# Pooled attention with a token-mixing layer on one core: PSUM banks chosen by expected release, wider sums of exponentials, two key buffers

## The chip, the cores and the metric

One core of a Trainium2 chip runs the whole program. Its engines work side by side and wait for each other by semaphores: TensorE (PE, with its weight loads listed as PEld), VectorE (DVE), ScalarE (ACT), GpSimd (POOL), and SyncE (SP), which here only starts transfers. The metric is the device time of one execution in microseconds; less is better.

## The reference

```python
q_pool = q.reshape(B, H, S // 2, 2, D).mean(axis=3)          # B, H = 8, 8; S = 1152; D = 64
scores = q_pool @ k^T / sqrt(D)                              # per head 576 x 1152
scores = scores - max(scores, axis=-1)
attn = exp(scores);  attn = attn / (sum(attn, -1) + 1e-9)
x = attn @ v, heads side by side                             # (8, 576, 512)
theta = x @ w_theta
y = w_tok_r @ (x * cos(theta)) + w_tok_i @ (x * sin(theta))  # over the 576 tokens
u = x + y
out = u + relu(u @ w_ch)
```

## The kernel before

The first stage is the attention. It goes over 32 pairs of heads (`NPAIR`), two heads side by side in the 128 partitions. A pair has two halves of the pooled queries (u = 0, 1; 288 columns each) and nine key tiles (kt = 0 to 8). What is done for a pair i:

- `load_q`, `load_k`, `load_v` start the transfers of queries, keys and values; `pool_q` (GpSimd) adds neighbouring queries.
- `prep_t` turns keys and pooled queries on TensorE (tiles `pt`, twice a pair, g = 0 and 1); `prep_hi` (ScalarE) and `prep_lo` (VectorE) split the result in two parts `hi` and `lo`.
- `maxpass` computes rough scores on TensorE (`pm`, twelve tiles a pair) and VectorE reduces each to maxima (L312). `max_tail` does the rest (`px`), `max_nm` and `max_row` (`pmt`, `mT`) turn the maxima, and `load_max` writes them as a row (`nmr`) by four small transfers.
- `escore` computes the exact scores for one u and kt in eight matmuls (`pe`, with the maximum subtracted in the fourth term), and ScalarE takes the exponential into `pc` (L374).
- `ssum` adds exponentials of kt = 0 to 7 on GpSimd (L383, `ss`); that of kt = 8 (`TAIL`) stays apart.
- `av` multiplies the exponentials with the values (`pa`, nine key tiles, two heads). `norm_sum` sums over the keys by matmuls with ones (L408). The `norm_` steps invert the sums by way of DRAM, multiply, and store.

Between these, `weights` fetches the 18 tiles of the later stage's weights step by step: several VectorE operations (L525 to L540), GpSimd (L542, L544, L555), and for token weights a turn on TensorE into `pwt` with splits by ScalarE and VectorE (L161, L164). The second stage (x to out, 8 batches) is left as it is.

The order on every engine is written by hand. Each step has a position in units of one `escore` (18 to a pair), in tables such as `PLAN`, `MAX_AT`, `AV_AT` and `W_AT`; all steps are sorted by it and each engine then takes them in that order. `burst(i, 0)` at position 10.35 holds the second `prep_all` of pair i+2, `max_row` of the next, `av`, and `norm_sum` of the pair before; `burst(i, 1)` at 19.25 holds `tail_prep` and the other `av`.

Results of matmuls go to PSUM, taken in double banks by `bank2`. There are four: two of kind "e" for `pe` and `pa`, two of kind "m" for all else, each kind used in turn. There are 14 buffers for exponentials and one for the keys (`kn`).

Of the kernel before, what the change touches and what calls it, by code (L numbers as in the profile page):

```python
# [9 lines left out]
F32 = mybir.dt.float32  # L10
# [7 lines left out]
EPS = 1e-9  # L18
TAIL = 8
PC_BUFS = 14  # L20
MAX_AT = (-24.9, -23.65, -22.55, -20.85, -19.55, -18.8, -15.55, -14.35, -13.5, -11.6, -10.2, -9.15)
# [10 lines left out]
    "load_q": -44.55,  # L32
    "load_k": -43.2,
    "pool_q": -35.35,
# [12 lines left out]
BANKS = {}  # L47
PAIRS = {"e": 2, "m": 2}
BANKS2 = {"h": 1, "t": 1, "m": 4, "r": 2}
# [42 lines left out]
def pooled_attention_moe_kernel(  # L92
# [51 lines left out]
    def bank(kind, name):  # L144
        pool, bufs = psum["now"]
        return pool.tile([P, 512], F32, tag=kind, name=name, bufs=bufs[kind])

    def bank2(kind, name):
        return psum["now"][0].tile([P, 2, 512], F32, tag=kind, name=name, bufs=PAIRS[kind])

# [37 lines left out]
    with ExitStack() as p1:  # L188
# [3 lines left out]
        )  # L192
        inp = p1.enter_context(tc.tile_pool(name="inp", bufs=1))
        opd = p1.enter_context(tc.tile_pool(name="opd", bufs=3))
# [26 lines left out]
        def load_k(i):  # L221
            b, hp = divmod(i, NP)
            h0 = 2 * hp
            kn = inp.tile([P, KT, 2, D], F32, tag="kn", name=f"kn{i}")
            for h in range(2):
                nc.sync.dma_start(kn[:, :, h, :], k[b, h0 + h].rearrange("(p t) d -> p t d", t=KT))
            state[i]["kn"] = kn
# [8 lines left out]
        def load_v(i):  # L236
            b, hp = divmod(i, NP)
            h0 = 2 * hp
            vn = inp.tile([P, 2, KT, D], F32, tag="vn", name=f"vn{i}", bufs=2)
            nc.sync.dma_start(vn, v[b, h0 : h0 + 2].rearrange("h (p t) d -> p h t d", t=KT))  # L240
            state[i]["vn"] = vn
# [10 lines left out]
        def prep_t(i, g):  # L252
            st = state[i]
            kn = st["kn"]
            pt = st["pt", g] = bank2("m", f"pt{g}_{i}")
            if g == 0:
# [39 lines left out]
        def maxpass(i):  # L296
# [4 lines left out]
            for j in range(4):  # L301
                for g in range(3):
                    pm = bank2("em"[g % 2] if i == 0 else "m", f"pm{i}_{j}{g}")
                    for h, hs in enumerate(HEADS):
                        nc.tensor.matmul(  # L305
                            pm[:, h, 0:W],
                            hi[hs, Q0 + j * P : Q0 + (j + 1) * P],
                            hi[hs, K0[3 * g] : K0[3 * g] + W],
                            start=True,
                            stop=True,  # L310
                        )
                    nc.vector.tensor_reduce(  # L312
                        mx[:, j : j + 5 : 4, g : g + 1], pm[:, :, 0:W], AX.X, ALU.max
                    )
                    yield

        def max_tail(i, pt):
            st = state[i]
            hi, tl, mx = st["hi"], st["tail"], st["mx"]
            pm = bank2("m", f"px{i}")  # L320
            for n, c, k, w in ((0, 0, 0, 4), (1, 0, 4, 2), (1, 2 * P, 6, 2)):
# [4 lines left out]
            if pt is None:  # L326
                pt = bank2("m", f"py{i}")
            nc.tensor.matmul(
# [10 lines left out]
        def max_row(i):  # L339
            st = state[i]  # L340
            px = bank2("m", f"pmt{i}")
            nc.tensor.transpose(out=px[0:KT, 0, 0:P], in_=st["nm"], identity=ident)
            mT = st["mT"] = sml.tile([KT, P], F32R, tag="mT", name=f"mT{i}")
            nc.scalar.copy(mT, px[0:KT, 0, 0:P])
            return px

# [7 lines left out]
        def escore(i, u, kt):  # L354
            st = state[i]
            hi, lo, nmr = st["hi"], st["lo"], st["nmr"]
            pcs = st.setdefault("pc", {})
            pcs[u, kt] = pch.tile([P, 2, HALF], F32, tag="pc", name=f"pc{i}_{u}{kt}")
            pe = bank2("e", f"pe{i}_{u}{kt}")
# [16 lines left out]
        def ssum(i, u, kt):  # L376
            st = state[i]
            if kt == 0 or kt >= TAIL:
                return
            if kt == 1:  # L380
                st["ss", u] = nrm.tile([P, 2, HALF], F32, tag=f"ss{u}", name=f"ss{u}_{i}", bufs=2)
            first = st["pc"][u, 0] if kt == 1 else st["ss", u]
            nc.gpsimd.tensor_tensor(st["ss", u], first, st["pc"][u, kt], ALU.add)  # L383

        def av(i, u):
            st = state[i]
            if u == 0:
                st["xu"] = nrm.tile([P, 2, HALF], F32, tag="xu", name=f"xu{i}", bufs=3)
            pa = bank2("e", f"pa{i}_{u}")
            for kt in range(KT):  # L390
# [10 lines left out]
        def norm_sum(i, px):  # L401
            st = state[i]
            sets = [[st["ss", u]] + [st["pc"][u, kt] for kt in range(TAIL, KT)] for u in range(2)]
            for n in range(len(sets[0])):
# [51 lines left out]
        def burst(i, u):  # L456
            if u == 0:
                if i + 2 < NPAIR:
                    prep_all(i + 2, 1)
                px = max_row(i + 1) if i + 1 < NPAIR else bank2("m", f"pmt{i}")  # L460
                av(i, u)
                if i > 0:
                    norm_sum(i - 1, px)
            else:
# [31 lines left out]
        def weights():  # L496
# [78 lines left out]
            def token(wv, kb, jt):  # L575
# [8 lines left out]
                yield  # L584
                pw2 = bank2("m", "pwt")
                pt = pw2[:, 0]
# [37 lines left out]
        def early():  # L624
            run(wgen)
            pw.close()
            xp0 = ctx.enter_context(tc.tile_pool(name="xp0", bufs=1, side="right"))
            xTs.append(xp0.tile([P, ND, 5 * P], F32, name="xT0"))
# [55 lines left out]
        for i in range(NPAIR):  # L684
            plan(i)
        at(NU * NPAIR + 2, 9, lambda: norm_sum(NPAIR - 1, bank2("m", "pend")))
        pw = ExitStack()
# [303 lines left out]
```

## Time and profile before

| | us |
|---|---|
| median of 3 runs | 1422.26 |
| lowest and highest | 1418.68, 1423.93 |
| span of the profiled execution, first to last instruction | 1414.8 |
| VectorE busy | 862.2 |
| ScalarE busy | 730.6 |
| GpSimd busy | 911.4 |

The time of the profiled execution outside its span is not listed; the median of the runs is 7.5 us more than the span. The attention takes the first 920 us of the span. A matmul row's length is from its start to its modelled end, and rows of neighbours overlap, so the start-to-start distance tells what an instruction costs TensorE.

### The profile page before, as it was taken

To read this page: it belongs to the slowest core of one execution; us is meant where nothing else is said; L and a number is where in the kernel's file an instruction comes from. 1 tells how busy PE (TensorE), PEld (TensorE's weight loads), DVE (VectorE), ACT (ScalarE), POOL (GpSimd) and SP (SyncE) were. 2 spreads that over 40 slices of the span, in tenths; PEclk is the share of its full clock that TensorE was granted. 3 is DMA by queue.
4 is the path that set the end of the run, shared out by engine and by line. 5 is a ranking of instruction groups with operands and counts; after the bars stand their busy time and mean duration, and the time that the engine had idled before them with its cause. 6 is when DMAs were issued, how large, how long until landed. Compare 5 with 4: busy or idle time off the path is not lost.

```text
span 1414.8 us, 29922 instructions
## 1 busy us (share of the span) xinstructions
PE 1352.8 (96%) x12178; PEld 1086.1 (77%) x12178; DVE 862.2 (61%) x1143; ACT 730.6 (52%) x1250; POOL 911.4 (64%) x672
## 2 busy tenths in 40 slices
PE   5999999999999999999999999999999999999998
PEld 4667676766676767767776766688999999999998
DVE  5866676777577767766687666355362553536442
ACT  2556465655555655556565655465444544445431
POOL 2789888978798889889898888834232413232210
PEclk7999999999999999999999999999999999999999
DMA  5224343434342443324343421231111211111111
GB/s 127 74 75 126 85 111 84 119 85 116 86 125 69 108 122 106 94 83 125 84 111 86 119 80 51 79 122 38 35 38 34 60 50 34 38 35 44 28 31 38
DMA packets 130906, 111.66 MB, mean 79 GB/s; under 512 B 95040, under 2 KB 95424, under 8 KB 130768
## 3 DMA queue, kind: packets, MB, share of 16 engines
q1 hardware_dynamic: 130592, 109.28, 28.0%
q8 instruction: 96, 1.57, 0.5%
q0 software_dynamic: 176, 0.46, 0.1%
q14 instruction: 42, 0.34, 0.1%
HBM read 88.29 MB, written 21.27 MB: 77 GB/s over the span
## 4 chain that ended last, share of the span: by engine, by line
PE 67%; DVE 15%; ACT 10%; DMA 3%; issue 3%; POOL 1%; SPq 0%; ACTq 0%; POOLq 0%; DVEq 0%
PE pa L392 16%; PE pe L371 16%; PE py L821 11%; PE pth L743 7%; PE pr L860 5%; DVE mx L312 5%; ACT pc L374 4%; PE pm L305 3%; PE pt L265 3%; PE pmt L408 2%; DMA kn<-in_k_dram 2%; DVE wf L532 1%; PE pxn L731 1%; DVE ws L530 1%; DVE lo L292 1%
## 5 line engine op out<-in xcount | busy, mean ns | idle before, releaser
L383 POOL TENSOR_TENSOR ss<-ss,pc 128x576 f32<-128x576 f32 x384 | 558.1, 1453 | 98.2 <-ACT pc L374 75.9
L312 DVE TENSOR_REDUCE mx<-pm 128x2 f32<-128x768 f32 x384 | 343.9, 950 | 134.8 <-PE pm L305 134.4
L374 ACT ACTIVATE pc<-pe 128x576 f32<-128x576 f32 x576 | 371.2, 652 | 102.2 <-PE pe L371 84.2
L392 PE MATMUL pa<-pc,vn 128*64 128x288 f32 x2304 | 293.5, 409 | 0.3 <-ACT pc L374 0.3
L794 POOL TENSOR_TENSOR Z<-ab,Z 128x512 fp32r<-128x512 f32 x40 | 52.2, 1305 | 306.0 <-ACT Z L790 277.8
L392 PEld LDWEIGHTS pa<-pc,vn 128*64 128x64 f32 x2304 | 159.7, 137 | 110.7 <-ACT pc L374 4.8
L821 PE MATMUL py<-wtk,Z 128*128 128x288 f32 x1728 | 241.7, 297 | 0.0
L821 PEld LDWEIGHTS py<-wtk,Z 128*128 128x128 f32 x1728 | 233.2, 189 | 1.3
L371 PE MATMUL pe<-hi 64*128 64x288 f32 x1152 | 203.1, 349 | 14.9 <-ACT pc L374 6.5
L371 PEld LDWEIGHTS pe<-hi 64*128 64x128 f32 x1152 | 108.3, 184 | 92.9 <-ACT pc L374 57.9
L371 PE MATMUL pe<-hi,lo 64*128 64x288 f32 x1152 | 170.8, 293 | 0.0
L371 PE MATMUL pe<-lo,hi 64*128 64x288 f32 x1152 | 170.8, 293 | 0.0
L371 PE MATMUL pe<-nmr,oner 64*128 64x288 f32 x1152 | 169.5, 290 | 0.0
L305 PE MATMUL pm<-hi 64*128 64x384 f32 x768 | 138.1, 359 | 14.6 <-DVE mx L312 8.6
L371 PEld LDWEIGHTS pe<-lo,hi 64*128 64x128 f32 x1152 | 109.8, 187 | 0.0
L371 PEld LDWEIGHTS pe<-hi,lo 64*128 64x128 f32 x1152 | 109.1, 186 | 0.0
L371 PEld LDWEIGHTS pe<-nmr,oner 64*128 64x128 f32 x1152 | 109.0, 185 | 0.0
L292 DVE TENSOR_TENSOR lo<-pt,hi 128x768 fp32r<-128x768 f32 x64 | 67.6, 1057 | 66.9 <-ACT hi L281 66.9
L860 PEld LDWEIGHTS pr<-us,wch 128*128 128x128 f32 x768 | 104.5, 188 | 2.0
L860 PE MATMUL pr<-us,wch 128*128 128x288 f32 x768 | 105.8, 295 | 0.0
L281 ACT CAST hi<-pt 128x768 fp32r<-128x768 f32 x64 | 56.2, 878 | 91.5 <-DVE mx L332 74.3
L383 POOL TENSOR_TENSOR ss<-pc,pc 128x576 f32<-128x576 f32 x64 | 93.8, 1466 | 3.0 <-ACT pc L374 3.0
(105 smaller groups left out, 1652.7 us busy)
## 6 DMA issues: line engine op xcount, KB each, us to landing
qn<-in_q_dram SPq DMA_DIRECT2D x32, 576.0 KB
kn<-in_k_dram SPq DMA_DIRECT2D x64, 288.0 KB
vn<-in_v_dram SPq DMA_DIRECT2D x32, 576.0 KB
dn<-ro SPq DMA_DIRECT2D x64, 144.0 KB
xd<-xu SPq DMA_DIRECT2D x32, 288.0 KB
xT<-xd SPq DMA_DIRECT2D x8, 1152.0 KB
out_dram<-on SPq DMA_DIRECT2D x23, 192.0 KB
out_dram<-on SPq DMA_DIRECT2D x23, 128.0 KB
```

The costliest lines, as they stand in the source:

```text
L281: nc.scalar.copy(hi, src)
L292: nc.vector.tensor_tensor(lo, src, hi.bitcast(F32), ALU.subtract)
L305: nc.tensor.matmul(pm[:, h, 0:W], hi[hs, Q0 + j * P : Q0 + (j + 1) * P], hi[hs, K0[3 * g] : K0[3 * g] + W], start=True, stop=True,)
L312: nc.vector.tensor_reduce(mx[:, j : j + 5 : 4, g : g + 1], pm[:, :, 0:W], AX.X, ALU.max)
L371: nc.tensor.matmul(pe[:, h, 0:HALF], w[hs], x[hs], start=(n == 0), stop=(n == 3))
L374: nc.scalar.activation(pcs[u, kt], pe[:, :, 0:HALF], AF.Exp, scale=SC)
L383: nc.gpsimd.tensor_tensor(st["ss", u], first, st["pc"][u, kt], ALU.add)
L392: nc.tensor.matmul(pa[hs, 0, 0:HALF], st["vn"][:, h, kt, :], st["pc"][u, kt][:, h, :], start=(kt == 0), stop=(kt == KT - 1),)
L743: nc.tensor.matmul(th, xs[c][:, j * P : (j + 1) * P], ws[:, c], start=(n == 0), stop=(n == 11))
L794: engine("zlo", b).tensor_tensor(Z[1], t, Z[0].bitcast(F32), ALU.subtract)
L821: nc.tensor.matmul(st["py", c, u][:, 0:HALF], Z[zi][:, c * P : (c + 1) * P], wtk[wi][:, kw, u * HALF : (u + 1) * HALF], start=(i == 0 and ...
L860: nc.tensor.matmul(pr[u][:, 0:HALF], wch[wi][:, c, e * P : (e + 1) * P], st["us", ui][:, c, u * HALF : (u + 1) * HALF], start=(n == 0), st ...
```

## The change

Three things change, all in the attention stage.

Banks: the two kinds are given up. A planner in `bank2` keeps a clock for TensorE, ScalarE and VectorE, and for each of four double banks the time at which it expects it free. Each tile takes the bank that comes free first. For each kind of tile `HOLD` has the TensorE work, the engines that read it (a: ScalarE, d: VectorE), and the time from then to its release. The order of work on the engines stays.

Sums: exponentials of an even and the following odd key tile now lie in one buffer (seven such buffers), that of kt = 8 in one of its own (`pl`, three buffers). GpSimd adds whole buffers, so that `ss` holds two sums side by side, and `norm_sum` sums three pieces by the ones matmul instead of two. `norm_sum` takes a bank of its own (`pns`) and doesn't share that of `max_row`.

Keys: there are two `kn` buffers, and `load_k` goes from position -43.2 to -43.62, ahead of `load_max`. The pool of the inputs goes to the other side of SBUF; `vn` changes its pool.

```diff
-TAIL = 8
-PC_BUFS = 14
+PC_BUFS = 7
-    "load_k": -43.2,
+    "load_k": -43.62,
-PAIRS = {"e": 2, "m": 2}
+SLOTS = 4
+HOLD = {
+    "e": (0.54, "a", 0.6),
+    "pm": (0.17, "d", 0.95),
+    "pt": (0.75, "ad", 2.1),
+    "px": (0.6, "d", 1.55),
+    "pa": (4.4, "a", 0.4),
+    "mt": (0.2, "a", 0.3),
+    "ns": (1.5, "a", 0.5),
+    "pw": (0.75, "ad", 1.9),
+}
...
+    clock = {"p": 0.0, "a": 0.0, "d": 0.0}
+    slots = [0.0] * SLOTS
     def bank2(kind, name):
-        return psum["now"][0].tile([P, 2, 512], F32, tag=kind, name=name, bufs=PAIRS[kind])
+        n = min(range(SLOTS), key=lambda k: slots[k])
+        work, engines, after = HOLD[kind]
+        clock["p"] = max(clock["p"], slots[n]) + work
+        end = max([clock["p"] + 0.3] + [clock[e] for e in engines]) + after
+        for e in engines:
+            clock[e] = end
+        slots[n] = end + 0.1
+        return psum["now"][0].tile([P, 2, 512], F32, tag=f"b{n}", name=name, bufs=1)
...
-            kn = inp.tile([P, KT, 2, D], F32, tag="kn", name=f"kn{i}")
+            kn = inp.tile([P, KT, 2, D], F32, tag="kn", name=f"kn{i}", bufs=2)
...
-            pcs[u, kt] = pch.tile([P, 2, HALF], F32, tag="pc", name=f"pc{i}_{u}{kt}")
+            if kt == KT - 1:
+                pcs[u, kt] = pch.tile([P, 2, HALF], F32, tag="pl", name=f"pl{i}_{u}", bufs=3)
+            elif kt % 2 == 0:
+                pw2 = st["pp", u, kt] = pch.tile([P, 2, 2, HALF], F32, tag="pc", name=f"pc{i}_{u}{kt}")
+                pcs[u, kt], pcs[u, kt + 1] = pw2[:, 0], pw2[:, 1]
...
-            if kt == 0 or kt >= TAIL:
+            if kt < 3 or kt % 2 == 0:
                 return
-            if kt == 1:
-                st["ss", u] = nrm.tile([P, 2, HALF], F32, tag=f"ss{u}", name=f"ss{u}_{i}", bufs=2)
-            first = st["pc"][u, 0] if kt == 1 else st["ss", u]
-            nc.gpsimd.tensor_tensor(st["ss", u], first, st["pc"][u, kt], ALU.add)
+            if kt == 3:
+                st["ss", u] = nrm.tile([P, 2, 2, HALF], F32, tag="ss", name=f"ss{u}_{i}", bufs=3)
+            first = st["pp", u, 0] if kt == 3 else st["ss", u]
+            nc.gpsimd.tensor_tensor(st["ss", u], first, st["pp", u, kt - 1], ALU.add)
...
-            sets = [[st["ss", u]] + [st["pc"][u, kt] for kt in range(TAIL, KT)] for u in range(2)]
+            sets = [[st["ss", u][:, n] for n in range(2)] + [st["pc"][u, KT - 1]] for u in range(2)]
```

Each call of `bank2` now names its kind of `HOLD`: "e" in `escore`, "pa" in `av`, "pm" in `maxpass`, and so on.

On SP, around the maxima of one pair (`nmr`), with the store of a finished pair (`xd`) and the loads behind it. Before:

```order
L351 DMA nmr_109<-mT_3580 1x4x128
L352 DMA nmr_109<-mT_3580 1x16x4
L351 DMA nmr_109<-mT_3580 1x4x128
L352 DMA nmr_109<-mT_3580 1x16x4
L491 DMA xd_83<-xu_2801 128x576
L226 DMA kn_3620<-in_k_dram 128x9x64 x2
L240 DMA vn_3634<-in_v_dram 128x2x576
```

and in the changed kernel:

```order
L246 DMA kn_3517<-in_k_dram 128x9x64 x2
L370 DMA nmr_109<-mT_3479 1x4x128
L371 DMA nmr_109<-mT_3479 1x16x4
L370 DMA nmr_109<-mT_3479 1x4x128
L371 DMA nmr_109<-mT_3479 1x16x4
L515 DMA xd_83<-xu_2722 128x576
L260 DMA vn_3537<-in_v_dram 128x2x576
```

The load of keys moved from behind the four transfers of the maxima and the store to ahead of them all.

On GpSimd, the sums of pair 9 with the pooling of queries (`qp`) and a weight step between them. Before:

```order
L383 TENSOR_TENSOR ss_9_3872<-ss_9_3872,pc_07_3890 128x576
L542 TENSOR_TENSOR raw<-raw 128x512
L383 TENSOR_TENSOR ss_9_4077<-pc_10_3922,pc_11_3941 128x576
L383 TENSOR_TENSOR ss_9_4077<-ss_9_4077,pc_12_4012 128x576
L383 TENSOR_TENSOR ss_9_4077<-ss_9_4077,pc_13_4035 128x576
L383 TENSOR_TENSOR ss_9_4077<-ss_9_4077,pc_14_4051 128x576
L544 TENSOR_TENSOR ws<-wf,raw 128x512
L383 TENSOR_TENSOR ss_9_4077<-ss_9_4077,pc_15_4066 128x576
L234 TENSOR_TENSOR qp_4140<-qn_3935 96x6x64 x2
L383 TENSOR_TENSOR ss_9_4077<-ss_9_4077,pc_16_4079 128x576
L555 TENSOR_TENSOR hl<-ws,hl 128x512
L383 TENSOR_TENSOR ss_9_4077<-ss_9_4077,pc_17_4095 128x576
```

and in the changed kernel:

```order
L406 TENSOR_TENSOR ss_9_3790<-ss_9_3790,pc_06_3765 128x1152
L566 TENSOR_TENSOR raw<-raw 128x512
L406 TENSOR_TENSOR ss_9_3996<-pc_10_3811,pc_12_3904 128x1152
L568 TENSOR_TENSOR ws<-wf,raw 128x512
L406 TENSOR_TENSOR ss_9_3996<-ss_9_3996,pc_14_3942 128x1152
L254 TENSOR_TENSOR qp_4026<-qn_3824 96x6x64 x2
L579 TENSOR_TENSOR hl<-ws,hl 128x512
L406 TENSOR_TENSOR ss_9_3996<-ss_9_3996,pc_16_3967 128x1152
```

Seven adds of a half became three of twice the width, and the first of them now needs the exponentials of four key tiles instead of two.

On TensorE, the ones matmul for pair 8 behind `pa` of pair 9, with `pe` of the next key tile behind it. Before:

```order
L408 MATMUL pmt_3966<-ss_8_3485,ones 32x288
L408 MATMUL pmt_3966<-ss_8_3687,ones 32x288
L408 MATMUL pmt_3966<-ss_8_3485,ones 32x288
L408 MATMUL pmt_3966<-ss_8_3687,ones 32x288
L408 MATMUL pmt_3966<-pc_08_3519,ones 32x288
L408 MATMUL pmt_3966<-pc_18_3721,ones 32x288
L408 MATMUL pmt_3966<-pc_08_3519,ones 32x288
L408 MATMUL pmt_3966<-pc_18_3721,ones 32x288
L371 MATMUL pe_12_4013<-hi_2992 128x288 x2
```

and in the changed kernel:

```order
L431 MATMUL pns_3879<-ss_8_3617,ones 32x288
L431 MATMUL pns_3879<-ss_8_3414,ones 32x288
L431 MATMUL pns_3879<-ss_8_3617,ones 32x288
L431 MATMUL pns_3879<-pl_0_3420,ones 32x288
L431 MATMUL pns_3879<-pl_1_3619,ones 32x288
L431 MATMUL pns_3879<-pl_0_3420,ones 32x288
L431 MATMUL pns_3879<-pl_1_3619,ones 32x288
L394 MATMUL pe_12_3905<-hi_2910 128x288 x2
```

Eight matmuls became twelve (the first five of the changed kernel, on `ss` too, are left out above), and their bank is no longer that of `pmt`.

## Rows read from the trace of the kernel before

**Rows 1.** The page: the span, and in the 40 equal slices of the span the busy share of TensorE in tenths.

```profile
span 1414.8 us, 29922 instructions
PE   5999999999999999999999999999999999999998
```

**Rows 2.** The chain of waits through one pair, from 700 to 729 us: start, length, what. `x8` counts matmuls of one `pe`, `x16` eight matmuls with their eight weight loads.

```profile
701.40 4.52 PE pa L392 x36
...
707.52 0.69 PE pe L371 x8
...
708.32 0.66 ACT pc L374
...
709.02 0.80 PE pe L371 x8
709.82 0.17 PE pm L305 x2
709.99 0.53 PE pe L371 x8
...
713.01 0.98 PE pt L265 x9
713.99 0.11 PE pmt L342
714.10 4.51 PE pa L392 x36
718.62 1.11 PE pmt L408 x16
...
726.87 0.81 PE pt L265 x6
727.68 0.47 PE px L322 x3
728.15 0.06 PE pt L328
728.21 4.51 PE pa L392 x36
```

**Rows 3.** Busy time of each engine from 73.20 to 853.20 us, from one `pa` of u=0 (pair 1) to that of pair 29: the stretch, its length, then busy time of PE, PEld, DVE, ACT and POOL with counts of instructions, the granted clock, the DMA share and GB/s.

```profile
73.20:853.20 780.00, 751.61 (x7774) 545.29 (x7773) 547.51 (x647) 446.40 (x770) 672.85 (x490) 1.00 0.37 100
```

**Rows 4.** Instructions in order of time, in the same plain half as rows 2: two exponentials, and three reductions to maxima.

```profile
709.92 1.35 ACT L374 ACTIVATE pc<-pe 128x576 f32<-128x576 f32 x2 [0.26 <-PE pe L371]
...
710.03 2.69 DVE L312 TENSOR_REDUCE mx<-pm 128x2 f32<-128x768 f32 x3 [0.47 <-PE pm L305]
```

**Rows 5.** Instructions of TensorE in order of time: `pa` at the start and behind the end of the first and the last of 13 halves of that kind (12.66 to 12.84 us from start to start).

```profile
87.48 4.59 PE L392 MATMUL pa<-pc,vn 128*64 128x288 f32 x36
100.18 4.59 PE L392 MATMUL pa<-pc,vn 128*64 128x288 f32 x36
...
840.57 4.59 PE L392 MATMUL pa<-pc,vn 128*64 128x288 f32 x36
853.24 4.59 PE L392 MATMUL pa<-pc,vn 128*64 128x288 f32 x36
```

**Rows 6.** The chain of waits behind a weight tile's turn (`pwt`).

```profile
747.08 0.12 PE pwt L597
...
747.85 0.70 DVE wtk L164
...
749.29 0.44 PE pm L305 x2
```

**Rows 7.** Instructions of TensorE in order of time: `pa` in the last halves of the attention.

```profile
892.29 4.59 PE L392 MATMUL pa<-pc,vn 128*64 128x288 f32 x36 [0.30 <-ACT pc L374]
903.89 4.59 PE L392 MATMUL pa<-pc,vn 128*64 128x288 f32 x36
```

**Rows 8.** All instructions of a line: count, then least, median and greatest length in ns; the adds of exponentials on GpSimd, and one of the weight operations on VectorE.

```profile
L383 POOL TENSOR_TENSOR ss<-ss,pc x384: 1390/1422/1940, 34.4 to 918.7; 128x576 f32<-128x576 f32 x192
```

```profile
L530 DVE TENSOR_SCALAR ws<-wf x18: 416/1402/2105, 58.0 to 857.7; 128x512 f32<-128x512 f32 x8, 128x576 f32<-128x576 f32 x8, 64x576 f32<-64x576 f32 x2
```

**Rows 9.** Instructions in order of time in the sum half that starts at 714.10: GpSimd's adds, and VectorE's maxima with a weight operation between them.

```profile
721.34 6.02 POOL L383 TENSOR_TENSOR ss<-ss,pc 128x576 f32<-128x576 f32 x4 [1.54 <-ACT pc L374]
```

```profile
720.67 1.82 DVE L312 TENSOR_REDUCE mx<-pm 128x2 f32<-128x768 f32 x2 [0.55 <-PE pm L305]
722.41 0.68 DVE L532 TENSOR_SCALAR wf<-ws 128x576 uint32<-128x576 uint32 x1
723.01 3.57 DVE L312 TENSOR_REDUCE mx<-pm 128x2 f32<-128x768 f32 x4
```

**Rows 10.** Instructions in order of time: a weight operation of VectorE between the maxima of a plain half, and the `pa` at the half's start and behind its end. Eleven plain halves have one there.

```profile
287.89 1.45 DVE L528 TENSOR_SCALAR wf<-raw 128x512 uint32<-128x512 uint32 x1
```

```profile
281.49 4.59 PE L392 MATMUL pa<-pc,vn 128*64 128x288 f32 x36
294.71 1.68 PE L392 MATMUL pa<-pc,vn 128*64 128x288 f32 x12
```

**Rows 11.** The chain of waits at a late load of keys, and from the list of who waited for whom between 100 and 900 us the row on keys (total, times, longest).

```profile
303.43 4.93 DMA kn<-in_k_dram
...
308.50 0.84 PE pt L265 x6
```

```profile
PE pt L265 <- DMA kn<-in_k_dram: 4.7, 7, 1.2
```

More of the change, by code (lines that the diff above doesn't have):

```diff
@@ L192, in pooled_attention_moe_kernel @@
         )
-        inp = p1.enter_context(tc.tile_pool(name="inp", bufs=1))
+        pi = ExitStack()
+        inp = pi.enter_context(tc.tile_pool(name="inp", bufs=1, side="right"))
         opd = p1.enter_context(tc.tile_pool(name="opd", bufs=3))
@@ L238, in load_v @@
             h0 = 2 * hp
-            vn = inp.tile([P, 2, KT, D], F32, tag="vn", name=f"vn{i}", bufs=2)
+            vn = opd.tile([P, 2, KT, D], F32, tag="vn", name=f"vn{i}", bufs=2)
             nc.sync.dma_start(vn, v[b, h0 : h0 + 2].rearrange("h (p t) d -> p h t d", t=KT))
@@ L254, in prep_t @@
             kn = st["kn"]
-            pt = st["pt", g] = bank2("m", f"pt{g}_{i}")
+            pt = st["pt", g] = bank2("pt", f"pt{g}_{i}")
             if g == 0:
@@ L302, in maxpass @@
                 for g in range(3):
-                    pm = bank2("em"[g % 2] if i == 0 else "m", f"pm{i}_{j}{g}")
+                    pm = bank2("pm", f"pm{i}_{j}{g}")
                     for h, hs in enumerate(HEADS):
@@ L319, in max_tail @@
             hi, tl, mx = st["hi"], st["tail"], st["mx"]
-            pm = bank2("m", f"px{i}")
+            pm = bank2("px", f"px{i}")
             for n, c, k, w in ((0, 0, 0, 4), (1, 0, 4, 2), (1, 2 * P, 6, 2)):
@@ L326, in max_tail @@
             if pt is None:
-                pt = bank2("m", f"py{i}")
+                pt = bank2("px", f"py{i}")
             nc.tensor.matmul(
@@ L340, in max_row @@
             st = state[i]
-            px = bank2("m", f"pmt{i}")
+            px = bank2("mt", f"pmt{i}")
             nc.tensor.transpose(out=px[0:KT, 0, 0:P], in_=st["nm"], identity=ident)
@@ L344, in max_row @@
             nc.scalar.copy(mT, px[0:KT, 0, 0:P])
-            return px
         def load_max(i):
@@ L388, in av @@
                 st["xu"] = nrm.tile([P, 2, HALF], F32, tag="xu", name=f"xu{i}", bufs=3)
-            pa = bank2("e", f"pa{i}_{u}")
+            pa = bank2("pa", f"pa{i}_{u}")
             for kt in range(KT):
@@ L459, in burst @@
                     prep_all(i + 2, 1)
-                px = max_row(i + 1) if i + 1 < NPAIR else bank2("m", f"pmt{i}")
+                if i + 1 < NPAIR:
+                    max_row(i + 1)
                 av(i, u)
                 if i > 0:
-                    norm_sum(i - 1, px)
+                    norm_sum(i - 1, bank2("ns", f"pns{i}"))
             else:
@@ L584, in token @@
                 yield
-                pw2 = bank2("m", "pwt")
+                pw2 = bank2("pw", "pwt")
                 pt = pw2[:, 0]
@@ L626, in early @@
             pw.close()
+            pi.close()
             xp0 = ctx.enter_context(tc.tile_pool(name="xp0", bufs=1, side="right"))
@@ L685, in pooled_attention_moe_kernel @@
             plan(i)
-        at(NU * NPAIR + 2, 9, lambda: norm_sum(NPAIR - 1, bank2("m", "pend")))
+        at(NU * NPAIR + 2, 9, lambda: norm_sum(NPAIR - 1, bank2("ns", "pend")))
         pw = ExitStack()
```

## Prediction

> **What bounds the kernel now.** I read the page first: TensorE is busy in nearly every slice, but its busy time includes waiting inside the pipeline, so it says little [rows 1]. The chain of waits through one ordinary pair says more [rows 2]. Call the stretch from one `pa` of u=0 to the `pa` of u=1 behind it the sum half (it starts with the ones matmul), and from there to the next `pa` of u=0 the plain half. The plain half starts at 701.40 and lasts 12.70 us, the sum half at 714.10 lasts 14.11. What TensorE must issue is less. Nine `pe` at 0.53 are 4.77 and six `pm` at 0.17 are 1.02. The plain half adds 4.52 (`pa`), 0.98 (`pt`) and 0.11 (`pmt`): 11.40. The sum half adds 4.51, 1.11 (ones), 0.81 (`pt`) and 0.53 (`px` with its last piece): 12.75. So about 1.3 us of each half is waiting, and the rows say on what: a `pe` ends, its exponential runs from 708.32 for 0.66, and only then the next-but-one `pe` starts at 709.02. With two double banks for `pe`, matmul, exponential and two handovers make a loop of 1.6 us for two `pe`. From 73.20 to 853.20 lie 28 pairs at 27.86 us [rows 3]; the ordinary pair needs 26.81, so about 29 us more go to odd halves: late key loads, weight tiles, VectorE work for the weights between the maxima.
>
> **Part 1, the banks.** Nothing is computed otherwise; a tile takes the one of four double banks that the table of expected holds calls free first. I followed the table's clocks by hand through a pair. In the plain half the third `pe` gets the bank of the first, the fourth that of the second; a `pm` mostly gets that of a `pm` two back; later ones mix, a `pe` behind a `pm` and the reverse. So TensorE still runs only about two tiles of each kind ahead. With 0.53 and 0.17 issued, 0.11 more for a `pe` behind a stall, 0.25 to the exponential, exponentials 0.675 apart and reductions 0.90 apart [rows 2, 4], the nine `pe` of the plain half start 0, 0.70, 1.49, 2.29, 2.82, 3.78, 4.59, 5.38 and 5.95 us behind the `pa`. Then `pt` comes at 6.48, `pmt` at 7.46, the next `pa` at 7.57, and that ends at 12.09. Against 12.68 in the undisturbed halves that is 0.59 gained. The same walk through the sum half, with the longer ones matmul (part 2) in it, ends at 14.05, against 14.10: 0.05 gained. VectorE is tighter there than now: its six reductions run without a gap from 2.5 to 8.2, and four tiles wait for one of them.
> - Undisturbed plain halves: 13 of 28 (the first starts at 87.48, the last at 840.57 [rows 5]): 13 x 0.59 = 7.7 gained.
> - Undisturbed sum halves: 7 x 0.05 = 0.4.
> - Ten weight tiles `pwt`: now `pwt` goes through ScalarE and VectorE twice while only one bank is left for `pm`, and the next `pm` starts 2.1 us behind its end [rows 6]. These halves are 0.7 to 2.0 us longer than ordinary ones; 0.71 of it is TensorE's own work. With four banks to choose from I give back half of the rest: about 4.
> - The last three halves have no `pm`; all four banks serve `pe`. 892.29 to 903.89 is 11.60 [rows 7] for 4.52 + 4.77 issued, so 2.3 of it is waiting. Exponentials need 9 x 0.675 = 6.1 of the 9.3, so TensorE can run ahead: 1.5 each, 4.5.
>
> **Part 2, sums over two key tiles.** Seven GpSimd adds of 128x576 at a median of 1.42 us [rows 8] become three of 128x1152. A wide one is between 1.42 (no cost by width, which no row supports) and 2 x 1.42 = 2.84 (all of it by width); I take 2.8. 7 x 1.42 = 9.9 becomes 8.4 a half, some 3 us a pair less of GpSimd. GpSimd is busy 673 of 780 us [rows 3] and is not what TensorE waits for in rows 2, so this is worth nothing by itself. The price is the ones matmul: `x16` counts eight matmuls and eight loads, 1.11 us in two rounds of four column groups [rows 2]. A third round is half of that, 0.5 to 0.56; it stands on TensorE's path, 32 x 0.51 = 16 us. In the sum halves it is already counted; the last one adds 0.5 at the end.
>
> **Part 3, where wide adds hurt.** The weight operations of VectorE that read and write SBUF have strange times: L530 takes 0.416 at least, 1.402 in the median, 2.105 at most [rows 8]. The excess is about what is left of a 1.4 us add: VectorE waits until GpSimd's instruction ends. The rows of one place agree: the VectorE operation at 722.41 needs 0.68 while four adds run from 721.34 [rows 9]. With 2.8 us adds the rest can be twice as long. The Trainium skill, page "SBUF — State Buffer", section "Who interferes with whom", says that the port pair shared by VectorE and GpSimd is an exclusive lock held for the whole instruction; by it this change would lengthen the worst of these waits, which is a rival below.
> - Eleven plain halves have such an operation behind their first reduction: 1.45 us at 287.89, and the half is 13.22 instead of 12.68 [rows 10]. In the changed kernel GpSimd has finished the previous half's adds there, by my walk at 0.3 us, and the next add needs the fourth exponential at 2.1. The operation (at 1.8) should mostly find it free and take 0.45. From a loss of 1.0 (a full wait) to a gain of 0.85, I take +0.6: 6.6.
> - Nine sum halves have one behind the second reduction (0.68 at 722.41 [rows 9]), which now costs nothing. In the changed kernel the first wide add starts with the fourth exponential at 3.77 us, the operation comes at 4.30, and the add runs to 6.57. A full wait delays the remaining reductions by 2.7 and the half ends 2.15 later than now; no wait costs nothing. I take -1.0: -9.
> - Operations behind the reductions are mostly covered by the 4.5 us of `pa`; -3 in all. If that cover fails the next `pm` waits for `lo`.
>
> **Part 4, two key buffers.** Now the load of the next keys is queued behind four `nmr` transfers and `xd`, and waits for the only buffer: a load starts at 303.43, lands 4.93 later, and `pt` follows at 308.50 at once [rows 11]. Seven such waits sum to 4.7 us on the matmuls, and five sum halves around them are 0.6 to 1.9 longer than ordinary (6.2 together). With the load ahead of the `nmr` transfers in the queue and a second buffer, it starts over 5 us earlier. What is late next in those halves is the ordinary chain: 5 gained, bounds 4.7 and 6.2. `nmr` behind it on SP waits for `mT` anyway, and nothing that is passed is needed sooner than 5 us later.
>
> **The sum.** 7.7 + 0.4 + 4 + 4.5 + 6.6 - 9 - 3 - 0.5 + 5 = 15.7, say 16 us. The profiled span of 1414.8 becomes 1399; 7.5 lie around it to the median of 1422.26, so 1406.
>
> **The rivals.**
> - *The banks decouple more than my walk shows* (gain). If waiting falls to 0.35 us a half instead of 0.7, 56 halves give 20 more, and if the nine sum halves lose nothing, 9 more: 1377. For it: four banks are as many as TensorE could ever use here. Against it: reductions in the sum half have no slack. Chance 0.18.
> - *Wide adds hold VectorE up* (slower; the rule named above makes it). All 20 operations between reductions meet a wide add: nine sum halves -2.15 (-19), eleven plain halves -1.0 instead of +0.6 (-11), late ones -8 instead of -3. With the other +21 that is 17 us lost: 1439. It decides from a mean wait of about 1.3 us for these 20 operations (no gain is left), and shows as VectorE's weight operations at up to 3.3 us. For it: the excess in the trace follows the add's length. Against it: GpSimd has more idle time, in particular at the plain half's operation. Chance 0.17.
> - *The banks do nothing beyond paying for the ones matmul* (no change): plain halves keep 12.5 as a mixed ring waits for the slower of two engines; keys and weight tiles pay for the waits on VectorE: 1422. Also the case if the release is not as expected and a `pe` stands behind a late reduction. Chance 0.20.
>
> **How the numbers follow.** Forecast 1406, chance 0.45, its own range 1393 to 1417. 0.5% is 7.1 us, about what a measurement of this kernel can tell from no change: under 1415.1 is faster, over 1429.4 slower. Faster: 0.18 and most (0.37) of the forecast, 0.55. Within: the rest of the forecast, the no-change case and a little of the slow one, 0.29. Slower: 0.16. The range 1380 to 1436 takes in the two middle cases and about half of each outer one.
>
> **What would show it.** In the changed profile: ordinary plain halves of 12.1 and sum halves of 14.0; the ones matmul at 1.6; adds at 2.8; no `pt` waiting for keys; halves with weight operations of VectorE between reductions at 12.4 (plain) and 14 to 16 (sum). I am wrong if plain halves stay at 12.7, or if sum halves with such an operation are two us longer throughout.

## The result, and the profile after

The changed kernel takes 1433.82 us (median of 4 runs, 1433.70 to 1434.56) and the kernel before 1420.47 (median of 4, 1416.92 to 1423.93). The ratio is 1.0099, with a 95% interval of 1.0078 to 1.012: slower by about 14 us, where the prediction had 16 us faster. The time lies inside the predicted range and beside the rival that ended at 1439: wide adds hold VectorE up. One run of `early_slot` (1634.23 us, at a granted clock of 0.75 where the other nine show 0.98 or 0.99) is left out of what follows.

The page of the changed kernel: its span, and GpSimd's wide adds with count, busy time and mean ns. The span was 1414.8 [rows 1]; an add of twice the width takes 1.87 times as long (median 2.66 against 1.42 us [rows 8]).

```profile
span 1431.9 us, 29706 instructions
...
L406 POOL TENSOR_TENSOR ss<-ss,pc 128x1152 f32<-128x1152 f32 x128 | 343.9, 2687 | 8.7 <-ACT pc L397 2.7
```

The changed kernel's busy time of each engine from `pa` of u=0 in pair 1 to that of pair 29, the columns of rows 3. The 28 pairs took 780.00 us and now 796.33, though GpSimd's busy time there fell from 672.85 to 554.86: as predicted, its load was not what TensorE waited for. VectorE's "busy" time rose by 26 us (547.51 to 573.33) with as many instructions: that is waiting inside instructions.

```profile
73.84:870.17 796.33, 759.91 (x7998) 562.24 (x7998) 573.33 (x646) 440.38 (x769) 554.86 (x266) 0.99 0.41 97
```

An ordinary pair is no slower. In the changed kernel's chain of waits (compare rows 2), the sum half runs from 297.17 to 311.28, 14.11 us, and the plain half from there to 323.55, 12.27. The ones matmul (`pns`) takes 1.59 instead of 1.11. There is no exponential left on the chain.

```profile
297.17 4.52 PE pa L415 x36
301.68 1.59 PE pns L431 x24
...
311.28 4.52 PE pa L415 x36
...
323.44 0.11 PE pmt L362
```

The loss is in halves where VectorE works on a weight tile. The instructions of VectorE, then of GpSimd, then the two `pa` of one of the nine sum halves (compare rows 9): the weight operation needs 0.4 to 0.5 us alone, comes 0.48 us after the first wide add has started, and takes 2.50. Four reductions queue behind it, and the half is 16.08 instead of 14.10.

```profile
191.59 1.82 DVE L332 TENSOR_REDUCE mx<-pm 128x2 f32<-128x768 f32 x2 [4.29 <-PE pm L325]
193.33 2.50 DVE L549 TENSOR_SCALAR raw<-raw 128x576 uint32<-128x576 uint32 x1
195.75 3.54 DVE L332 TENSOR_REDUCE mx<-pm 128x2 f32<-128x768 f32 x4
```

```profile
192.85 2.66 POOL L406 TENSOR_TENSOR ss<-pc,pc 128x1152 f32<-128x1152 f32 x1 [6.96 <-ACT pc L397]
195.59 2.75 POOL L406 TENSOR_TENSOR ss<-ss,pc 128x1152 f32<-128x1152 f32 x1
```

```profile
184.46 4.10 PE L415 MATMUL pa<-pc,vn 128*64 128x288 f32 x32 [0.24 <-PE pmt L362]
...
200.54 4.10 PE L415 MATMUL pa<-pc,vn 128*64 128x288 f32 x32
```

The second place is a late operation, behind the last reduction of a half. Three plain halves that start under one of 4.3 to 4.8 us are 2.5 to 3.0 us longer than before. One of them, 337.59 to 353.87, takes 16.28 us; the same half was 13.25 in the kernel before. VectorE, then GpSimd: the operation at 337.51, the second of two, lasts 4.80 us, through `qp` and the whole add behind it.

```profile
336.21 1.38 DVE L549 TENSOR_SCALAR raw<-raw 128x576 uint32<-128x576 uint32 x1
337.51 4.80 DVE L552 TENSOR_SCALAR wf<-raw 128x576 uint32<-128x576 uint32 x1
```

```profile
337.23 2.18 POOL L254 TENSOR_TENSOR qp<-qn 96x384 f32<-96x384 f32 x2
339.38 2.61 POOL L406 TENSOR_TENSOR ss<-ss,pc 128x1152 f32<-128x1152 f32 x1
```

The chain of waits there: `pa`, which starts at 337.59 and takes 4.59 us, covers all but about 0.1 us of the operation, and the maxima of `px`, `hi` and `lo` then stand bare in front of the next `pm`.

```profile
337.59 4.72 DVE wf L552
342.32 1.13 DVE mx L351
...
343.68 0.81 ACT hi L301
...
344.51 0.97 DVE lo L312
...
345.61 0.69 PE pm L325 x2
346.31 0.96 PE pe L394 x8
```

All instructions of the line that rows 8 show in the kernel before: the median falls from 1.402 to 0.460 us and the greatest rises from 2.105 to 3.958. Most operations find GpSimd idle now, and the few that don't pay more.

```profile
L554 DVE TENSOR_SCALAR ws<-wf x18: 414/460/3958, 58.7 to 874.9; 128x512 f32<-128x512 f32 x8, 128x576 f32<-128x576 f32 x8, 64x576 f32<-64x576 f32 x2
```

The list of who waited for whom: waits for keys are left only at the start (12.4 us in 8 before, over the whole span, 7.7 of it at the start).

```profile
PE pt L285 <- DMA kn<-in_k_dram: 7.9, 1, 7.9
```

### The profile page after: what moved, and what is told of

Read it like the earlier page. It is cut to its first block, busy times and chain, and to the rows that moved or that the text cites. A ratio compares the mean times of both kernels' runs of the same rounds, so it can differ in the third digit from the quotient of the medians.

```text
span 1431.9 us, 29706 instructions
## 1 busy us (share of the span) xinstructions
PE 1362.0 (95%) x12434; PEld 1104.0 (77%) x12434; DVE 894.7 (62%) x1143; ACT 723.0 (50%) x1250; POOL 775.5 (54%) x416
## 4 chain that ended last, share of the span: by engine, by line
PE 70%; DVE 17%; ACT 5%; DMA 4%; issue 2%; POOL 1%; SPq 1%; ACTq 0%; POOLq 0%; DVEq 0%
PE pe L394 18%; PE pa L415 16%; PE py L846 11%; PE pth L768 6%; PE pr L885 5%; DVE mx L332 5%; PE pm L325 4%; PE pt L285 4%; PE pns L431 3%; DVE wf L552 1%; DMA ro<-rc 1%; DVE ws L554 1%; PE pxn L756 1%; DVE raw L549 1%; DVE r L790 1%
## 5 line engine op out<-in xcount | busy, mean ns | idle before, releaser
L332 DVE TENSOR_REDUCE mx<-pm 128x2 f32<-128x768 f32 x384 | 348.5, 952 | 129.2 <-PE pm L325 128.3
L397 ACT ACTIVATE pc<-pe 128x576 f32<-128x576 f32 x512 | 324.9, 652 | 83.7 <-PE pe L394 80.2
L406 POOL TENSOR_TENSOR ss<-ss,pc 128x1152 f32<-128x1152 f32 x128 | 343.9, 2687 | 8.7 <-ACT pc L397 2.7
L406 POOL TENSOR_TENSOR ss<-pc,pc 128x1152 f32<-128x1152 f32 x64 | 171.6, 2681 | 236.2 <-ACT pc L397 236.2
L415 PE MATMUL pa<-pc,vn 128*64 128x288 f32 x2048 | 262.5, 409 | 0.8 <-PE pmt L362 0.7
L415 PEld LDWEIGHTS pa<-pc,vn 128*64 128x64 f32 x2048 | 143.6, 137 | 97.0 <-issue 4.7
L394 PE MATMUL pe<-lo,hi 64*128 64x288 f32 x1152 | 174.4, 297 | 0.0
L394 PE MATMUL pe<-nmr,oner 64*128 64x288 f32 x1152 | 173.3, 295 | 0.0
L394 PEld LDWEIGHTS pe<-hi 64*128 64x128 f32 x1152 | 111.7, 188 | 75.2 <-ACT pc L397 28.9
L325 PEld LDWEIGHTS pm<-hi 64*128 64x128 f32 x768 | 75.7, 192 | 47.1 <-DVE mx L332 25.6
```

The lines of the kernel that those rows point to most:

```text
L325: nc.tensor.matmul(pm[:, h, 0:W], hi[hs, Q0 + j * P : Q0 + (j + 1) * P], hi[hs, K0[3 * g] : K0[3 * g] + W], start=True, stop=True,)
L332: nc.vector.tensor_reduce(mx[:, j : j + 5 : 4, g : g + 1], pm[:, :, 0:W], AX.X, ALU.max)
L394: nc.tensor.matmul(pe[:, h, 0:HALF], w[hs], x[hs], start=(n == 0), stop=(n == 3))
L397: nc.scalar.activation(pcs[u, kt], pe[:, :, 0:HALF], AF.Exp, scale=SC)
L406: nc.gpsimd.tensor_tensor(st["ss", u], first, st["pp", u, kt - 1], ALU.add)
L415: nc.tensor.matmul(pa[hs, 0, 0:HALF], st["vn"][:, h, kt, :], st["pc"][u, kt][:, h, :], start=(kt == 0), stop=(kt == KT - 1),)
```

## The experiments

Two theories. **A**: a wide add keeps VectorE's weight operations out for its whole length, and the halves that meet one pay. **B**: the ring of four banks is at fault, since a `pe` can stand behind a late reduction. A third, **C**, is that the wide sums hurt through their larger buffers and later start, not through an instruction's length. The kernel before is run beside each; a ratio is to it.

### The old adds, and wide adds in two halves

`narrow_adds`: the changed kernel with the seven adds of 128x576 and two pieces into the ones matmul; banks and keys stay.

```diff
-            if kt < 3 or kt % 2 == 0:
+            if kt == 0 or kt >= TAIL:
...
-            nc.gpsimd.tensor_tensor(st["ss", u], first, st["pp", u, kt - 1], ALU.add)
+            nc.gpsimd.tensor_tensor(st["ss", u], first, st["pc"][u, kt], ALU.add)
```

> The changed kernel with its new banks and two key buffers, but with the sums of exponentials as before: seven GpSimd adds of 128x576, key tile 8 apart, two pieces to the ones matmul. Theory A (the wide add holds VectorE's weight operations up for its whole length): those operations fall from up to 4.8 us to under 2.2, sum halves with one between the maxima fall from 16.05 to 14.1 or less, ordinary sum halves lose a round of the ones matmul (14.11 to 13.6), plain halves stay at 12.24; 1390 us, between 1380 and 1402. Theory B (the mixed ring of banks is at fault, a late reduction now stops the exact scores too): only the ones matmul is saved, 16 us, and the disturbed halves stay long; 1410 to 1420 us.

`split_adds`: the changed kernel, each wide add as two of half the width; buffers and the three-piece ones matmul stay.

```diff
-            nc.gpsimd.tensor_tensor(st["ss", u], first, st["pp", u, kt - 1], ALU.add)
+            for n in range(2):
+                nc.gpsimd.tensor_tensor(
+                    st["ss", u][:, n], first[:, n], st["pp", u, kt - 1][:, n], ALU.add
+                )
```

> The changed kernel with each add of 128x1152 written as two adds of 128x576, one for each of the two sums side by side; buffers, three pieces, banks and keys as in the changed kernel. Theory A (the length of one GpSimd instruction is what VectorE waits out): VectorE's weight operations are at most 2.2 us, and the time is that of narrow_adds plus the third round of the ones matmul, 16 us: 1396 to 1418 us. Theory C (the later start of the sums, behind four exponentials, or the larger buffers are at fault): it stays at 1430 to 1436 us.

Measured: `narrow_adds` 1392.59 us, 0.9797 (0.9768 to 0.9826); `split_adds` 1404.43, 0.9882 (0.9853 to 0.991). In `narrow_adds` VectorE's operation of the sum half above takes 0.69 instead of 2.50:

```profile
186.35 0.69 DVE L546 TENSOR_SCALAR raw<-raw 128x576 uint32<-128x576 uint32 x1
```

The nine sum halves lie 3.1 us in all under the kernel before (changed kernel: 20.7 over it), and 28 pairs take 757.19 us:

```profile
71.74:828.93 757.19, 739.63 (x7774) 546.11 (x7773) 544.23 (x647) 441.49 (x769) 674.76 (x490) 1.00 0.43 102
```

By the ratios, on 1420 us: banks and keys give 29 us, the wide sums' buffers and third ones round take 12 back, and the length of the add another 31; together the 14 us lost. `split_adds` has the wide buffers and the late start, so C can explain no more than the 12, and the ordinary sum half accounts for those: 14.11 against 13.73 us in `narrow_adds`, 0.38 times 32.

The longest waits were not as A had them. One weight operation of `narrow_adds` takes 2.40 us and eight of `split_adds` take 2.5 to 3.6, where at most 2.2 was expected; all nine pass through `qp`. The other hundred of `split_adds` take at most 1.68 us.

### Old banks, and the wide sums alone

`old_banks`: the changed kernel with two double banks for `pe` and `pa`, two for the rest.

```diff
-        n = min(range(SLOTS), key=lambda k: slots[k])
...
+        tag = "e" if kind in ("e", "pa") else "m"
+        return psum["now"][0].tile([P, 2, 512], F32, tag=tag, name=name, bufs=2)
```

> The changed kernel with wide adds and two key buffers, but with the two kinds of banks of the kernel before. Theory A: the wide adds cost as much or more there and the gain of the banks (0.45 us in a plain half, the third round paid in a sum half) is gone: 1440 to 1455 us, ordinary plain halves 12.7, sum halves 14.6. Theory B: without the mixed ring the disturbed halves are short again, and the ones matmul less the late keys is left: 1425 to 1434 us.

`wide_only`: the kernel before with the wide sums alone.

```diff
-            nc.gpsimd.tensor_tensor(st["ss", u], first, st["pc"][u, kt], ALU.add)
+            nc.gpsimd.tensor_tensor(st["ss", u], first, st["pp", u, kt - 1], ALU.add)
```

> The kernel before with only the wide sums (seven paired buffers, three adds of 128x1152, three pieces to the ones matmul): two kinds of banks, one key buffer, load_k at its old position. Theory A: slower than before by the ones matmul (16 us) and the longer waits of VectorE (10 to 25 us): 1445 to 1462 us. Theory B: slower by the ones matmul alone, 1434 to 1440 us.

Measured: 1476.65, 1.0368 (1.0304 to 1.0433), and 1476.93, 1.0382 (1.0341 to 1.0423). B falls: with the old banks the wide adds cost more, 54 us on the kernel before (60 on `keys_only`, below) instead of the 43 that separate the changed kernel from `narrow_adds`. Both came out above what A had expected. A's nine sum halves are the same there (20.7 and 20.0 us over the kernel before); the surplus lies elsewhere, 23.7 and 14.1 us over it in the eleven plain halves and 3.0 in the seven clean sum halves. With the new banks TensorE can work ahead while VectorE is held; that is the reading, and it was not separated further.

### Keys alone, banks alone

`keys_only` (two buffers, and the load moved ahead) and `banks_only` (the bank by expected release) put one part each on the kernel before.

```diff
-            kn = inp.tile([P, KT, 2, D], F32, tag="kn", name=f"kn{i}")
+            kn = inp.tile([P, KT, 2, D], F32, tag="kn", name=f"kn{i}", bufs=2)
```

> The kernel before with only the two key buffers and the earlier load (adds, ones matmul and the two kinds of banks as before). If the keys are worth what the long sum halves showed (five halves by about 1.2 us), 1413 to 1417 us. Rival: the keys carry most of the 28 us that narrow_adds gained, 1395 to 1405 us.

```diff
-        return psum["now"][0].tile([P, 2, 512], F32, tag=kind, name=name, bufs=PAIRS[kind])
+        n = min(range(SLOTS), key=lambda k: slots[k])
...
+        return psum["now"][0].tile([P, 2, 512], F32, tag=f"b{n}", name=name, bufs=1)
```

> The kernel before with only the banks assigned by expected release (and a bank of its own for the ones matmul); adds, ones matmul and one key buffer as before. If the banks carry the rest: plain halves 12.3, sum halves 13.7, 1397 to 1402 us. Rival: without the second key buffer the earlier TensorE waits for keys in most sum halves and loses the gain, 1408 to 1418 us.

Measured: keys 1412.41, 0.9948 (0.993 to 0.9967), 7 us gained; banks 1416.22, 0.9973 (0.996 to 0.9987), 4 us. Together (`narrow_adds`) they give 29, far more than the two apart. For the banks the trace shows why: alone, TensorE reaches the keys' transposes earlier and waits 25.0 us for keys instead of 12.4 (below). What the keys alone meet next was not looked for; that it is the old banks is a reading.

```profile
PE pt L286 <- DMA kn<-in_k_dram: 25.0, 11, 7.8
```

### The dose: adds of half the width

`halved_adds`: the adds of `narrow_adds`, each as two of 128x288.

```diff
+            for h in range(2):
+                nc.gpsimd.tensor_tensor(
+                    st["ss", u][:, h], first[:, h], st["pc"][u, kt][:, h], ALU.add
+                )
```

> narrow_adds with every add of 128x576 written as two of 128x288 (fourteen a half): the opposite dose of the wide add. Theory A: VectorE's weight operations wait at most 0.8 us, halves with one behind a reduction come near the ordinary ones (plain 13.5 to 12.8), GpSimd is busy a little longer; 1380 to 1389 us. Rival: not the length of one instruction but GpSimd's total occupation counts, which grows: 1391 to 1400 us.

Measured: 1471.74, 1.0365 (1.0336 to 1.0394). Both theories missed by 70 us or more, and A as first put (a wait is the rest of one add) does not hold here. Eleven halves are 5.0 to 8.6 us longer than in `narrow_adds`, which makes 71 of the 76 us between the first and the last `pa`; each of them meets an operation of VectorE that lasts 6.0 to 11.5 us. VectorE's operations, then GpSimd's adds of 0.8 us, from 60 to 72 us: the operation that comes at 62.01 gets no turn at some ten boundaries between adds, and ends at 70.33, when the last of them (to 69.78) is over.

```profile
62.01 8.32 DVE L560 SCALAR_TENSOR_TENSOR wf<-raw,wf 128x512 uint32<-128x512 uint32 x1
```

```profile
60.71 3.06 POOL L404 TENSOR_TENSOR ss<-ss,pc 128x288 f32<-128x288 f32 x4
63.73 1.55 POOL L404 TENSOR_TENSOR ss<-pc,pc 128x288 f32<-128x288 f32 x2
65.25 4.53 POOL L404 TENSOR_TENSOR ss<-ss,pc 128x288 f32<-128x288 f32 x6
```

In this order each add depends on the one but last (the other head), not on the last; here such neighbours are called independent. `halved_chained` keeps the adds and their size, and puts all seven of a head behind one another, so that each waits for the last; it starts them only with the eighth exponential.

```diff
-            if kt == 0 or kt >= TAIL:
+            if kt != TAIL - 1:
...
+            for h in range(2):
+                for t in range(1, TAIL):
+                    first = st["pc"][u, 0] if t == 1 else ss
+                    nc.gpsimd.tensor_tensor(ss[:, h], first[:, h], st["pc"][u, t][:, h], ALU.add)
```

> halved_adds with its 128x288 adds in another order: all seven of one head first, each reading the sum that the one before wrote, then seven of the other head, started when key tile 7 is there. In halved_adds neighbours don't depend on each other, and VectorE waited through up to ten of them. If it is the independence of neighbours that keeps VectorE out, its weight operations now wait at most about 0.8 us (0.4 to 1.3 in all) and the time is under 1425 us. If it is the shortness of an add, waits of 5 us and more stay and the time is over 1450 us.

Measured: 1478.56 in one run (1418.30 for the kernel before). Of its 108 weight operations on VectorE the longest takes 1.35 us (8.33 in `halved_adds`). GpSimd, then VectorE, at the same place of the program: the operation ends while GpSimd's run of chained adds goes on to 64.04.

```profile
58.47 5.57 POOL L404 TENSOR_TENSOR ss<-ss,pc 128x288 f32<-128x288 f32 x6
```

```profile
61.75 0.75 DVE L558 SCALAR_TENSOR_TENSOR wf<-raw,wf 128x512 uint32<-128x512 uint32 x1
```

So short adds don't keep VectorE out by being short. But independence does not decide either, as the trace of `split_adds` shows: there too each add depends on the one but last, and VectorE gets in at the first boundary. VectorE, then GpSimd: the operation comes in the first of two independent adds (1.4 us each) and ends at 147.14, inside the second.

```profile
145.66 1.48 DVE L555 TENSOR_SCALAR wf<-raw 128x576 uint32<-128x576 uint32 x1
```

```profile
145.40 3.00 POOL L407 TENSOR_TENSOR ss<-pc,pc 128x576 f32<-128x576 f32 x2 [2.28 <-ACT pc L397]
```

In `split_adds` 33 operations of VectorE got in like this at the first boundary between two adds, and one (an `xu` multiply of 4.07 us at 869.01) did not; in `halved_adds` itself 39 got in, and 95 of its 108 weight operations take at most 1.45 us. What the traces of all thirteen kernels show is this: where GpSimd's next instruction waited for the last, VectorE got in at that boundary every time; where it did not wait, VectorE mostly got in and sometimes did not. What decides there stays open.

The time of `halved_chained` lies where the other theory had it, for a reason of its own by the trace: the late adds hold the exponentials' buffers, and ScalarE waits for them 86.8 us (2.8 in the kernel before).

```profile
ACT pc L394 <- POOL ss L404: 86.8, 56, 7.0
```

### Where the operations fall

`early_slot` moves one turn of the weight work from 12.75 to 11.2.

```diff
-W_AT = (9.45, 9.5, 9.85, 10.5, 12.75, 18.0, 18.6, 19.25, 20.45)
+W_AT = (9.45, 9.5, 9.85, 10.5, 11.2, 18.0, 18.6, 19.25, 20.45)
```

> The changed kernel, wide adds kept, with one position of the weight steps moved from 12.75 to 11.2, so that VectorE takes the operation one reduction earlier in the sum half, at about 3.4 us, ahead of the wide add that starts at 3.8. Theory A (it is the meeting with the add that costs): the nine sum halves fall from 16.05 by 1 to 1.7 each, 1415 to 1424 us. Rival: the operation waits for a wide add wherever it stands, 1429 to 1438 us.

`no_adds` has only the first wide add of each half.

```diff
-            if kt < 3 or kt % 2 == 0:
+            if kt != 3:
```

> The changed kernel with only the first wide add of each half left in; the second and the third are left out, so that the sums lack key tiles 4 to 7 and the output is scaled wrongly. Banks, keys, buffers and the twelve ones matmuls as in the changed kernel. Theory A (GpSimd's adds hold VectorE up, all else is sound): VectorE's weight operations are mostly 0.4 to 0.8 us, halves with one between the maxima are at most 0.5 longer than the ordinary 14.1 and 12.2, except those nine sum halves that still meet the first add; 1405 to 1418 us. Theory B (the ring of banks makes the long halves): 1428 to 1436 us.

`narrow_late` is `narrow_adds` with the last turn moved to the front.

```diff
-W_AT = (9.45, 9.5, 9.85, 10.5, 12.75, 18.0, 18.6, 19.25, 20.45)
+W_AT = (9.2, 9.45, 9.5, 9.85, 10.5, 12.75, 18.0, 18.6, 19.25)
```

> narrow_adds with one position of the weight steps moved from 20.45 (behind the first reduction of a plain half) to 9.2 (behind its last), where `pa` covers it. What is left of the loss in plain halves there (13.5 instead of 12.3 in about five, 14.0 in about six where the operation before it counts too) should shrink: 1383 to 1390 us. If the operations are only met by another wait at the new place, 1391 to 1396 us.

Measured: `early_slot` 1422.85, 1.0026 (1.0015 to 1.0037); `no_adds` 1414.37, 0.9976 (0.996 to 0.9992); `narrow_late` 1389.42, 0.9802 (0.9786 to 0.9817). The first two remove one of the two losses each:

| us against the kernel before | changed | `early_slot` | `no_adds` | `narrow_adds` |
|---|---|---|---|---|
| nine sum halves, operation behind the second reduction | +20.7 | +2.9 | +21.3 | -3.1 |
| eleven plain halves with one | +7.0 | +17.7 | -8.2 | +1.3 |

In `early_slot` the operation comes between the first and second reduction, ahead of the wide add, and is free; the later operations of the same tile then start earlier too and meet other adds. Here, in `early_slot`, is the operation of the sum half shown above, now 0.45 instead of 2.50, and a later one of the same tile, 4.68:

```profile
191.82 0.45 DVE L549 TENSOR_SCALAR raw<-raw 128x576 uint32<-128x576 uint32 x1
...
197.97 4.68 DVE L554 TENSOR_SCALAR ws<-wf 128x576 f32<-128x576 f32 x1
```

In `no_adds` the first add still stands in the sum half's way, and no add stands behind the reductions:

```profile
191.43 2.51 DVE L549 TENSOR_SCALAR raw<-raw 128x576 uint32<-128x576 uint32 x1
...
197.32 0.45 DVE L552 TENSOR_SCALAR wf<-raw 128x576 uint32<-128x576 uint32 x1
```

For `narrow_late` the intervals overlap with those of `narrow_adds`, so moving the turn shows no difference. Both are about 2% faster than the kernel before and 3% faster than the changed kernel.

## Why the prediction was wrong

Profiled spans: 1399 predicted, 1431.9 measured, 33 us apart. Each term, from the starts of `pa` in both traces, by the same halves (gain positive, us):

| term | predicted | measured |
|---|---|---|
| 13 ordinary plain halves | +7.7 | +5.6 |
| 7 ordinary sum halves, third ones round in them | +0.4 | 0.0 |
| weight tiles `pwt` | +4 | +3.2 |
| last three halves | +4.5 | +5.1 |
| keys | +5 | +3.0 |
| 9 sum halves with a VectorE operation | -9 | -20.7 |
| 11 plain halves with one, and late operations | +6.6 - 3 | -7.0 |
| other halves, before and behind the attention | -0.5 | -6.3 |

**The walk over the banks was right, to 0.15 us a half.** 12.09 and 14.05 were forecast for the ordinary halves, 12.24 and 14.11 came; the old plain half was 12.70. (The loop of 1.6 us for two `pe` is 1.50 in rows 2, from 707.52 to 709.02; no term uses it.) The third ones round was taken at 0.51 and is 0.48 in itself (1.59 against 1.11), of which 0.38 reach the path.

**The step that failed is Part 3: it took -1.0 for a sum half whose full wait it had priced at 2.15, and -3 for all late operations.** For the sum halves the walk put the operation at 4.30 us, inside an add from 3.77 to 6.57, and priced a full wait at 2.15 a half. The trace has just that: in the sum half shown above `pa` ends at 189.06, the add runs from 3.79 to 6.45 us behind that, and the operation comes at 4.27. The nine halves lose 1.7 to 3.4 each, 2.3 in the mean. The prediction then took -1.0, about half, although the order of the program is fixed and the same in all nine; there was nothing to average over. Six of them lie at 1.7 to 2.0 each, three at 2.7 to 3.4.

The count of nine was short, too: by the trace twelve sum halves have an operation behind their second reduction. The three others stand in other rows of the table: the first half (1.3 us longer), one that grew by 3.6, and one of the five of the keys' row (17.25 us; 14.30 in `early_slot`), without which that row would be +4.3, near the 4.7 to 6.2 of Part 4. In `narrow_adds` the three take 12.59, 16.25 and 13.74 us, against 14.45, 19.64 and 17.25. The operation in the second of them took 0.92 us in the kernel before:

```profile
393.88 2.89 DVE L554 TENSOR_SCALAR ws<-wf 128x576 f32<-128x576 f32 x1
```

Part 3 also read each excess as the rest of one add. The greatest of rows 8 is 2.105 - 0.416 = 1.69 us, more than the whole 1.42 of an add, and the trace of the kernel before has the reason: such waits went through the pooling of queries, past the boundary between its two instructions. VectorE, then GpSimd; it is the same operation that lasts 4.80 us in the changed kernel:

```profile
336.41 2.23 DVE L528 TENSOR_SCALAR wf<-raw 128x576 uint32<-128x576 uint32 x1
```

```profile
336.13 2.19 POOL L234 TENSOR_TENSOR qp<-qn 96x384 f32<-96x384 f32 x2
```

**The plain halves were half right.** The operation behind the first reduction mostly takes 0.42 instead of 1.45 [rows 10], as forecast, as in the row here, with the wide add only behind it:

```profile
290.87 0.42 DVE L552 TENSOR_SCALAR wf<-raw 128x512 uint32<-128x512 uint32 x1
```

```profile
291.70 2.67 POOL L406 TENSOR_TENSOR ss<-pc,pc 128x1152 f32<-128x1152 f32 x1 [3.05 <-ACT pc L397]
```

Five of the eleven gain 0.56 to 0.80 (0.6 was the term). Three lose 0.5 to 0.6 and three lose 2.5 to 3.0; these six start under a late operation of 3.9 to 4.8 us. "Mostly covered by `pa`" was the false cover: it holds 4.5 us, and a 3 us chain of `px` maxima, `hi` and `lo` has to follow the operation. That was named as the risk ("if that cover fails the next `pm` waits for `lo`") and given no price. `no_adds` separates the two terms: with no add behind the reductions the eleven halves gain 8.2, so the +6.6 was of the right size, and the late operations cost about 15 us in these halves (8.2 + 7.0, an estimate) where -3 was taken.

**The rival was right in mechanism, and in two of its three places.** It said nine sum halves at 19 (20.7), late operations at 8 (about 15), eleven plain halves at 11 for the operation between reductions (that one did not happen), and operations of up to 3.3 us (4.8). Its condition, a mean wait of 1.3 us for 20 operations, was judged against GpSimd's idle time; but an operation doesn't arrive at random, it arrives where the order of the program puts it. The Trainium skill, page "SBUF — State Buffer", section "Who interferes with whom", whose lock held for a whole instruction made this rival, says also that `tensor_reduce` never contends on this chip. The trace agrees: the reductions of 128x768 take 952 ns in the mean beside wide adds, 950 before.

**What was not foreseen.** Behind the last `pa` 3.4 us more pass, since `xu` of the last pair waits for a DMA on VectorE and the next stage's work is queued behind it. That cause was read from the chain and not tried.

## What to carry to other kernels

Where an instruction of one engine can keep another engine out, price each meeting from the order of the program: if the walk puts the operation inside the other's instruction, take the full wait, in every repetition, and count the repetitions in the trace. Fewer and wider instructions on an engine that is off the path are not free if a shorter one on the path has to wait for it; here the add's length cost 31 us and saved nothing on the path. Shorter ones are not safe by themselves: `halved_adds` was 52 us slower than the kernel before. And cover is a number of microseconds: compare it with the longest wait and the chain that has to follow, not with the usual wait.

## What the hardware did that I had not expected

**VectorE can wait through several GpSimd instructions.** Where GpSimd's next instruction depended on the last, the wait ended at that boundary (2.50 us at 193.33, under the chained wide adds). Where it did not, some waits went on: 2.23 us through the two of `qp` in the kernel before, 4.80 through `qp` and an add, 8.32 past ten boundaries between adds, and 14.42 for an `xu` multiply of `halved_adds`. Others ended at the first boundary all the same: 1.48 us at 145.66 in `split_adds`, and ten operations of `halved_chained` that got in where the first add of the second head follows the last of the first. The rule of the Trainium skill on the lock, named in the prediction, speaks of a single instruction. The waits of the weight operations of `split_adds` on its adds (at most 1.68 us) agree with it; the longer ones go beyond it. What decides whether VectorE gets in between independent instructions is not shown by these runs.

**A bare wait costs TensorE's clock as well.** Stretches of the changed kernel around the wait at 337.59, with the granted clock as the third column from the right: TensorE is busy 0.70 of 3.40 us, and then runs at 0.50, the lower of its levels (1.2 GHz), for the next 1.4 us and part of the 2 us behind them.

```profile
342.20:345.60 3.40, 0.70 (x8) 0.48 (x9) 2.54 (x5) 1.66 (x3) 0.00 (x0) 0.91 0.00 0
345.60:347.00 1.40, 1.39 (x10) 1.40 (x12) 1.02 (x3) 0.00 (x0) 0.00 (x0) 0.50 0.07 3
347.00:349.00 2.00, 2.00 (x23) 2.00 (x22) 1.82 (x4) 1.01 (x2) 0.97 (x1) 0.64 0.05 16
```

In the chain above, the `pe` behind it takes 0.96 instead of 0.53, as does the next one: with `pm` about 1.2 of that half's 3.0 us (an estimate: 0.43 more for each of the two `pe`, 0.15 more for each of the two `pm`). The other two halves of this kind show the fall too, a little later behind their waits (0.50 from 495.8 to 498.0, 0.51 from 639.6 to 642.0).
